# Quartering the token tiles' first products, with a new table of places for every operation

## The chip, the cores and the metric

The kernel runs on one core of one Trainium2 chip. The metric is the device time of one execution in microseconds. Engines are named as in the profile: PE is TensorE (PEld its weight loads), DVE is VectorE, ACT is ScalarE, POOL is GpSimd and SP is SyncE, which issues the DMAs.

## The reference

Attention that keeps the 32 largest scores of each query, and behind it a block that every token passes: two products with a softmax-weighted activation and a layer norm between them.

```python
# q, k, v: (8, 8, 576, 64)
scores = scale * np.matmul(q, k.transpose(0, 1, 3, 2))
kth = np.partition(scores, -32, axis=-1)[..., -32:-31]
scores = np.where(scores >= kth, scores, -1000000000.0)
attn = exp(scores - max); attn /= sum + 1e-09
x = np.matmul(attn, v)                      # -> (4608 tokens, 512)
h = x @ w_in                                # (4608, 1024)
sm = exp(h - max) / (sum + 1e-9)
solu = h * sm
ln = (solu - mean) / sqrt(var + 1e-06) * g_ln
out = ln @ w_out                            # (4608, 512)
```

The weights come as float64 and everything is computed in float32.

## The kernel before

**Attention.** Heads are taken in pairs, four pairs to each of the 8 batches. Of the 576 queries of a batch, 512 form four tiles of 128, and the remaining 64 of two heads fill one more. A step (32 in all, four to a batch) takes two pairs and two query tiles: steps 0 and 1 of a batch do tiles 0 and 1 with pairs 0, 1 and then 2, 3; steps 2 and 3 do tiles 2 and 3. In a step, `scores` (L2216) multiplies queries with keys on PE into PSUM, 64 contraction rows at a time, two matmuls side by side on the upper and lower half of the array; `evac` (L2227) copies the result with ACT. `count0` and `count1` (ACT Sign, DVE compare) count how many scores lie above a moving threshold; `nearest` and `best` (L2312, L2323) find the 16 values nearest to it, from which `kth` picks the 32nd largest. `exps` (L2348) takes exponentials on ACT, `keep` (L2393) zeroes what is below the 32nd on DVE. `transpose_p` (L2470) turns the result on PE, `copy_p` (L2483) copies it, `attn_v` (L2526) multiplies with the values on half the array's columns, two matmuls side by side, and `attn_t` (L2535) adds the last 64 keys. `copy_v` (L2549, L2556) scales the outcome on DVE into `xTm` or `xTt`, which hold x transposed, one slice to each head pair.

**Tokens.** 36 token tiles of 128 (four to a batch, one more for the left-over queries of every second batch) go through `mm1` (L2567, h = x @ w_in, two halves of 512 columns, each a sum over the four head pairs), `hexp` (L2578, ACT), `solu` (L2586, DVE), `square` (L2596, ACT), `spread` and `ln` (POOL), `transpose_ln` (L2617), `copy_ln` (L2623), `mm2` (L2628, two halves of the 1024 rows), `store` (ACT) and `send` (SP). A float32 matmul is two instructions in the trace. The PSUM tile `h` is one of two buffers named "big", and the scores use the same two. While a token's sum is open, until `solu` has read it, the scores have the other one.

**Weights.** 16 chunks are loaded as float64 words; DVE (`w_bits`, `w_corr`) and PE (`w_sum`, L1981) make float32 of them, and `w_copy` puts them into `w_in` (chunks 0 to 7: chunk 2 * pair + half) and `w_out`. At the end they are loaded again and checked.

**What sets the order.** The program of every engine is written out by a planner at build time and is then fixed. `work_of` lists all operations, each with an engine, a duration in ns, an extra time until its result lands (`late`), the operations it comes after and the buffers that it uses. `arranged` goes through them like a simulation: on each engine it looks at the operations whose inputs and buffers can be had, keeps those that could start within `PATIENCE` ns of the earliest of them, and issues the one with the smallest place. Places are the numbers of the table `PLACES` (L778), one for every operation. `TURN` adds ns where PE changes between the whole array ("f"), half the rows ("r", the scores) and half the columns ("c", attn_v). So the table decides between operations, and data decide what it can choose from. Only the order comes out of the planner; on the chip an engine takes its instructions in that order and waits at each for its semaphores.

A second program for inputs that the first cannot treat stands behind a check (`general_path`), and is not executed here.

Of the kernel before, what the change touches and what calls it, by code (L numbers as in the profile page):

```python
# [442 lines left out]
class Work:  # L443
# [6 lines left out]
    def add(self, key, engine, ns, after=(), uses=(), late=0, mode=None):  # L450
# [7 lines left out]
TURN = {("r", "f"): 150, ("f", "r"): 180, ("c", "f"): 205, ("f", "c"): 145,  # L458
        ("r", "c"): 180, ("c", "r"): 180}
# [34 lines left out]
def work_of(B, NP, steps, NF, w_wide):  # L494
# [7 lines left out]
    add = w.add  # L502
# [7 lines left out]
    for b in range(B):  # L510
        for hp in range(NP):
            n = pair(b, hp)
            add(("load_k", n), "SP", 950, behind("load_k", n), [("km", n)], late=2300)
# [11 lines left out]
    for i, (b, chunks) in enumerate(steps):  # L525
# [3 lines left out]
        add(("load_q", i), "SP", 1150, behind("load_q", i), [("q", i)], late=2300)  # L529
# [108 lines left out]
    for m, (b, t, x, made) in enumerate(tokens):  # L638
        for half in range(2):
            ready = made + ([("mm1", m - 1, u) for u in range(2)] if m else []) + [ready_of(c) for c in range(half, 8, 2)]  # L640
            add(("mm1", m, half), "PE", 3480, ready, [x, ("big", ("h", m))], mode="f")
        free = [("w_sum", 15)] if m == 1 and w_wide else []
        add(("hexp", m), "ACT", 1007, free + [("mm1", m, 0), ("mm1", m, 1)], [("big", ("h", m)), ("e", m), ("solu", m)], 115)
# [56 lines left out]
def arranged(work, rank):  # L700
# [23 lines left out]
    while len(start) < len(ops):  # L724
# [56 lines left out]
        -339758, -12781, -25208, -27877, 37731, 233358, 296, 105051, 96218, 90025, 178978, 252902,  # L781
        244000, 268551, 386938, 415275, 391135, 450403, 490825, 467595, 536751, 620389, 565976,
        679127, 740719, 661851, 783898, 770731, 790228, 893927, 893785, 963266,
    ],
    "load_t": [
        -80025, -31145, 36300, 49546, 49494, 80911, 88940, 148972, 157187, 191399, 204618, 265303,
        242814, 379090, 332469, 458214, 479052, 406643, 515896, 540675, 515666, 668938, 671843,
        720581, 717982, 793192, 742027, 827758, 819520, 890032, 913039, 961682,
    ],
    "load_v": [  # L790
        5319, 1480, 51022, 45481, 188816, 144910, 179523, 153830, 308475, 246135, 333153, 327154,
        412030, 463265, 437640, 432012, 583103, 575722, 599884, 559552, 638124, 712663, 704767,
        749478, 828294, 823974, 856710, 843393, 969577, 973661, 982483, 1008016,
    ],
    "prep_t": [
        -61945, -87345, 26278, 19638, -8730, 123415, 112043, 64876, 197393, 203082, 209099,
        243285, 345702, 316325, 405050, 432741, 494037, 489994, 501941, 520044, 617082, 642835,
        681846, 688123, 761106, 717329, 792500, 787155, 909850, 920002, 957331, 948603,
    ],
    "prep_tc": [  # L800
        4338, 31729, 74439, 103211, 71892, 81529, 72919, 101742, 164515, 194340, 295053, 275591,
        364723, 341559, 415389, 407627, 461137, 438553, 503629, 486164, 631436, 665358, 673210,
        709654, 759555, 758129, 786441, 814781, 916829, 948853, 939851, 972581,
    ],
    "prep_k": [
        -60943, -63278, -70349, -26069, -42273, -8750, 127523, 59000, 243742, 222705, 246805,
        237589, 361575, 400598, 401099, 421797, 472374, 488858, 508262, 574786, 637110, 675577,
        651769, 709906, 752064, 690701, 778193, 843688, 919829, 948201, 942202, 976495,
    ],
    "prep_kc": [  # L810
        4386, 1259, 123243, 137096, 118230, 85986, 126740, 91080, 220993, 187701, 233433, 204820,
        376470, 380016, 398731, 436516, 487070, 463318, 479133, 561124, 640742, 660501, 650085,
        710914, 775148, 783534, 778524, 835240, 922803, 1013798, 954303, 988974,
    ],
    "key_square": [
        -4807, -10479, 66029, 137082, 107576, 118285, 100863, 99055, 254747, 223927, 219983,
        241887, 382074, 399900, 389837, 454608, 479887, 488157, 529275, 515189, 644860, 690979,
        690863, 719751, 737841, 761871, 779678, 864903, 916172, 907344, 975895, 1000571,
    ],
    "tail_square": [  # L820
        26929, 14605, 100013, 137131, 136063, 58308, 80392, 79370, 239575, 272229, 246883, 251581,
        308867, 311986, 422199, 446864, 515800, 468069, 496456, 535239, 638456, 682141, 683618,
        672660, 775588, 750923, 772211, 791047, 855138, 930345, 971291, 966358,
    ],
    "key_stats": [
        92348, -19748, 26035, 15202, 122190, 113992, 181544, 108957, 246207, 243025, 253021,
        288772, 408504, 419434, 373738, 411187, 494000, 466874, 543467, 571921, 654056, 667583,
        687366, 699046, 765262, 778703, 806677, 825191, 868806, 1026195, 947557, 979604,
    ],
    "load_q": [  # L830
        -59271, -10584, 162877, 208999, 217746, -8934, 78975, 113377, 212835, 187676, 290008,
        301140, 284434, 326724, 436860, 497003, 414204, 458642, 518992, 564916, 579785, 620846,
        720192, 679914, 758251, 783803, 740037, 850815, 909964, 906235, 929596, 981195,
    ],
    "prep_q": [
        -52938, -38118, 56938, 77044, -59554, 85219, 162709, 142989, 215771, 247729, 278667,
        316160, 380350, 357086, 442926, 462694, 491000, 518228, 547128, 562615, 640425, 655851,
        698990, 730851, 735544, 760091, 823699, 888865, 908286, 923741, 969433, 1014055,
    ],
    "prep_qc": [  # L840
        5438, 63366, 52446, 134767, 64136, 75161, 195035, 183808, 242849, 287460, 293191, 371510,
        425968, 364349, 488763, 476329, 465356, 525184, 499437, 614146, 626301, 699742, 698545,
        745735, 768636, 779604, 840926, 877014, 945804, 930997, 952200, 1033695,
    ],
    "query_square": [
        63169, 84418, 69142, 92064, 62677, 75066, 191341, 120686, 227118, 285294, 276140, 342226,
        401444, 383473, 418081, 451775, 479613, 516395, 563335, 580962, 631937, 667102, 657175,
        748447, 762133, 776709, 773949, 878639, 892717, 939130, 971775, 1057944,
    ],
    "estimate": [  # L850
        -83506, 127952, 79019, 27039, 105930, 180710, 89736, 42838, 243394, 306540, 313101,
        342801, 413707, 436191, 458562, 488897, 502885, 576495, 566964, 582618, 653574, 699822,
        722473, 753711, 782087, 850158, 856146, 880647, 959006, 991084, 1003644, 1011006,
    ],
    "length": [
        55390, 64287, 21492, 142925, 91820, 89828, 187422, 189102, 225343, 302444, 316321, 331213,
        430746, 450075, 467065, 483618, 443843, 521081, 600380, 589002, 638944, 706432, 747530,
        730429, 775752, 832366, 866032, 877201, 961113, 983506, 1018506, 1066670,
    ],
    "root": [  # L860
        99246, 101551, 133489, 76502, 153437, 159993, 328449, 258282, 273277, 322044, 312402,
        345682, 435376, 421796, 426558, 489636, 494032, 574332, 622205, 621698, 663835, 788227,
        724548, 699723, 787574, 869704, 806750, 895189, 992785, 957593, 981899, 1024982,
    ],
    "begin": [
        11137, 56722, 26318, 141798, 82875, 187369, 201720, 176412, 273406, 321410, 278640,
        361581, 425447, 451800, 489085, 488954, 519027, 611009, 600940, 647109, 684366, 701264,
        752228, 758419, 793179, 851495, 882821, 921112, 988338, 1009069, 981779, 1020470,
    ],
    "scores": [  # L870
        [-59418, -45149, -46228, -36187, -85715, -39882, -83465, -59766, -61961],
        [82657, 60941, 68216, 26269, 63090, 61996, 26242, 61177, 58723],
        [87860, 87901, 87890, 62437, 67835, 57982, 159959, 48482, 69765],
        [84367, 83743, 155862, 144031, 34877, 75359, 128841, 135567, 145817],
        [71537, 53849, 68902, 132976, 59114, 118037, 68873, 110264, 107915],
        [141646, 97925, 94716, 134455, 142943, 99507, 191485, 186882, 96824],
        [152938, 191224, 59110, 197551, 203891, 215510, 127964, 202152, 197201],
        [226026, 229460, 237313, 237035, 187502, 187736, 192780, 199624, 198798],
        [269141, 275943, 254553, 254580, 277300, 269126, 277259, 275937, 249924],
        [281479, 298728, 285432, 289527, 294726, 285129, 283716, 304085, 288903],  # L880
        [308491, 308764, 338739, 339201, 342891, 346940, 344779, 346918, 317824],
        [378407, 372124, 377700, 364058, 378360, 351114, 351045, 365023, 349059],
        [417154, 412522, 383108, 385009, 415137, 411709, 389678, 392676, 380697],
        [419351, 419391, 429554, 429553, 450301, 450306, 439041, 439011, 405453],
        [466428, 468152, 464816, 466680, 475154, 473635, 454060, 453530, 452872],
# [353 lines left out]
    ],  # L1239
    "spread_r": [  # L1240
        [61416, 70137],
        [85209, 91923],
        [131370, 129488],
    ],
    "copy_s": [
# [1498 lines left out]
```

## Time and profile before

| | us |
|---|---|
| median of 3 runs | 1195.1 (1193.06 to 1195.21) |
| the profiled execution | 1193.35, span 1191.5 |
| PE busy | 1143.5 (96%) |
| DVE busy | 1054.0 (88%) |
| ACT busy | 1014.4 (85%) |
| POOL busy | 154.4 (13%) |
| mm2 (L2628), 576 matmul instructions, busy | 258.2 |
| mm1 (L2567), 512 and 64 instructions, busy | 229.2 and 28.8 |
| scores (L2216), half rows, 1024 instructions, busy | 169.1 |
| transposes of P (L2470), 1024 instructions, busy | 153.1 |
| attn_v (L2526), half columns, 1024 instructions, busy | 136.1 |

Busy times of an engine are the time in which at least one of its instructions runs. Matmuls overlap (one starts before the one before has left the array), so what a group costs PE is read from the start of it to the start of the next group, not from its durations. The granted clock is the share of TensorE's full clock that the chip's throttle allows.

### The profile page before, as it was taken

How to read it: one execution, taken by the hardware profiler on the slowest of the kernel's cores; microseconds unless marked ns; L12 is line 12 of the kernel's file. 1: busy time of each engine (PE TensorE's matmuls, PEld its weight loads, DVE VectorE, ACT ScalarE, POOL GpSimd, SP SyncE). 2: the span in 40 equal slices, each digit the busy share in tenths (PEclk: the TensorE clock that was granted, in tenths of full speed). 3: DMA queues.
4: the chain of work that ended last, by engine and by line, in shares of the span. 5: the costliest groups of instructions: out<-in, count | busy, mean ns of one | idle time of the engine just before them, and what ended most of it. 6: DMA issues, size and time to landing. Idle time of an engine off the chain costs nothing.

```text
span 1191.5 us, 18863 instructions
## 1 busy us (share of the span) xinstructions
PE 1143.5 (96%) x5868; PEld 648.2 (54%) x5868; DVE 1054.0 (88%) x3113; ACT 1014.4 (85%) x2180; POOL 154.4 (13%) x169
## 2 busy tenths in 40 slices
PE   6689999999999999999999999999999999999997
PEld 3345455555555555555555655555555555555553
DVE  4999999999899999899979998899989888999821
ACT  7899798999988898999896998999877989988642
POOL 1101101102021020202031010211013001120110
PEclk9799999999999999999999999999999999999999
DMA  7323111012110122111120112111020101102521
GB/s 202 97 75 92 43 34 48 13 49 54 59 26 28 33 63 65 37 45 40 51 54 12 40 49 68 31 41 52 30 76 18 42 21 40 59 11 91 173 76 30
DMA packets 110408, 64.55 MB, mean 54 GB/s; under 512 B 89421, under 2 KB 97882, under 8 KB 110298
## 3 DMA queue, kind: packets, MB, share of 16 engines
q1 hardware_dynamic: 110298, 63.25, 18.8%
q8 instruction: 49, 0.80, 0.3%
q14 instruction: 61, 0.50, 0.1%
HBM read 53.65 MB, written 9.57 MB: 53 GB/s over the span
## 4 chain that ended last, share of the span: by engine, by line
PE 50%; DVE 27%; ACT 17%; issue 3%; POOL 2%; DMA 0%; DVEq 0%; ACTq 0%; POOLq 0%
PE o_ps L2628 14%; PE h_ps L2567 9%; PE s_ps L2216 9%; ACT sg L2291 7%; PE tp_p L2470 6%; PE om L2526 6%; DVE junkv L2234 6%; DVE w L2323 5%; DVE w L2312 5%; DVE E L2393 3%; ACT PT L2483 2%; DVE solu L2586 2%; ACT X L2227 2%; PE tp_ln L2617 2%; PE om L2535 2%
## 5 line engine op out<-in xcount | busy, mean ns | idle before, releaser
L2628 PE MATMUL o_ps<-w_out,lnT 128*128 128x512 f32 x576 | 258.2, 594 | 0.2
L2567 PE MATMUL h_ps<-w_in,xTm 128*128 128x512 f32 x512 | 229.2, 593 | 0.0
L2323 DVE MAX8 w<-w 128x8 f32<-128x288 f32 x576 | 223.3, 445 | 0.2
L2291 ACT ACTIVATE sg<-X,t 128x576 bf16<-128x576 f32 x256 | 196.4, 774 | 12.0 <-DVE t L2276 10.8
L2312 DVE SCALAR_TENSOR_TENSOR w<-X,al,sg 128x576 f32<-128x576 f32 x256 | 200.7, 813 | 0.8
L2393 DVE SCALAR_TENSOR_TENSOR E<-X,kth,E 128x576 f32<-128x576 f32 x256 | 199.1, 815 | 1.6
L2227 ACT ACTIVATE X<-s_ps 128x576 f32<-128x576 f32 x256 | 160.2, 661 | 25.0 <-PE s_ps L2216 22.5
L2234 DVE TENSOR_SCALAR_CACHE_REDUCE junkv<-X,t 128x576 bf16<-128x576 f32 x216 | 174.6, 808 | 7.6 <-ACT X L2227 1.5
L2216 PE MATMUL s_ps<-kT,qT 64*128 64x288 f32 x1024 | 169.1, 438 | 9.8 <-ACT X L2227 4.4
L2628 PEld LDWEIGHTS o_ps<-w_out,lnT 128*128 128x128 f32 x576 | 105.1, 190 | 112.4 <-issue 110.1
L2470 PE MATMUL tp_p<-ident,E 128*128 128x128 f32 x1024 | 153.1, 278 | 7.9 <-DVE E L2393 2.9
L2483 ACT COPY PT<-tp_p 128x512 f32<-128x512 f32 x256 | 147.0, 591 | 12.4 <-PE tp_p L2470 11.9
L2470 PEld LDWEIGHTS tp_p<-ident,E 128*128 128x128 f32 x1024 | 116.3, 141 | 65.4 <-issue 31.8
L2348 ACT ACTIVATE E<-X 128x1152 f32<-128x1152 f32 x128 | 149.1, 1183 | 1.4 <-PE tp_p L2470 1.2
L2567 PEld LDWEIGHTS h_ps<-w_in,xTm 128*128 128x128 f32 x512 | 93.3, 190 | 98.1 <-issue 95.7
L2526 PE MATMUL om<-PT,vm 128*64 128x320 f32 (+1 forms) x1024 | 136.1, 411 | 1.0 <-ACT osb L2635 0.9
L2186 POOL TENSOR_TENSOR zs<-zs,phalf 128x9 f32<-128x9 f32 x32 | 63.6, 1989 | 520.2 <-DVE zs L2180 520.2
L2216 PEld LDWEIGHTS s_ps<-kT,qT 64*128 64x128 f32 x1024 | 85.7, 186 | 68.3 <-issue 22.2
L2526 PEld LDWEIGHTS om<-PT,vm 128*64 128x64 f32 x1024 | 69.9, 136 | 54.6 <-issue 10.6
L2602 POOL TENSOR_SCALAR var<-var 128x1 f32<-128x1 f32 x36 | 13.0, 361 | 490.3 <-ACT e_sb L2596 490.1
L2596 ACT ACTIVATE e_sb<-solu,nmu 128x1024 f32<-128x1024 f32 x36 | 41.5, 1153 | 23.1 <-DVE nmu L2590 21.8
L2578 ACT ACTIVATE e_sb<-h_ps 128x1024 f32<-128x1024 f32 x36 | 36.7, 1020 | 20.0 <-PE h_ps L2567 19.7
(146 smaller groups left out, 1503.9 us busy)
## 6 DMA issues: line engine op xcount, KB each, us to landing
km<-in_k_dram SPq DMA_DIRECT2D x32, 256.0 KB
q_sb<-in_q_dram SPq DMA_DIRECT2D x64, 128.0 KB
vm<-in_v_dram SPq DMA_DIRECT2D x32, 256.0 KB
out_dram<-osb SPq DMA_DIRECT2D x32, 256.0 KB
scales<-rows SPq DMA_DIRECT2D x58, 128.0 KB
w_raw<-in_moe_w_in_dram SPq DMA_DIRECT2D x8, 512.0 KB
w_raw<-in_moe_w_out_dram SPq DMA_DIRECT2D x8, 512.0 KB
w_again<-in_moe_w_in_dram SPq DMA_DIRECT2D x8, 512.0 KB
```

The lines of the kernel that those rows point to most:

```text
L2216: nc.tensor.matmul(out=s[:, n, 0:SH], lhsT=queries_of(i, t)[hd, :], rhs=kT[hd, k0 : k0 + SH], start=True, stop=True,)
L2227: nc.scalar.activation(out=x, in_=st[i].pop(("s", j))[:, :, 0:SH], func=AF.Copy, scale=scale,)
L2234: nc.vector.tensor_scalar(out=junk, in0=x_of(i, j), scalar1=st[i][t][:, j : j + 1], scalar2=None, op0=ALU.is_ge, op1=ALU.add, accum_out=co ...
L2291: nc.scalar.activation(out=d["sg", j], in_=x_of(i, j), func=AF.Sign, scale=-(1.0 + 2.0**-23), bias=d["t1"][:, j : j + 1], accum_out=column ...
L2312: nc.vector.scalar_tensor_tensor(out=w, in0=x_of(i, j), scalar=d["al"][:, j : j + 1], in1=d.pop(("sg", j)), op0=ALU.subtract, op1=ALU.mult,)
L2323: nc.vector.max(w8[:, j, 8 * half : 8 * half + 8], w[:, half * SH : (half + 1) * SH])
L2393: nc.vector.scalar_tensor_tensor(out=e, in0=x_of(i, j), scalar=d["kth"][:, j : j + 1], in1=e, op0=ALU.is_ge, op1=ALU.mult, accum_out=den_a ...
L2470: nc.tensor.transpose(tp[:, c, :], e[:, c * P : (c + 1) * P], ident)
L2483: nc.scalar.copy(out=dst, in_=st[i].pop(("tp", j)))
L2526: nc.tensor.matmul(out=o[h * D : (h + 1) * D, cols], lhsT=vm[:, h, c, :], rhs=pt[:, h * NM + c, :], start=(c == 0), stop=False,)
L2567: nc.tensor.matmul(out=h[:, half, :], lhsT=x[:, c, :], rhs=w_in[:, c, half * 512 : (half + 1) * 512], start=(c == 0), stop=(c == NP - 1),)
L2628: nc.tensor.matmul(out=o, lhsT=d["lnT"][:, c, :], rhs=w_out[:, c, :], start=(c == 0), stop=(c == NF - 1),)
```

## The change

It has four parts.

1. `mm1` comes in four operations to a token instead of two. Operation `quarter` adds two head pairs' rows (`two` = 0 or 1: pairs 0, 1 or pairs 2, 3) into one half of the columns (`half`). It is listed as waiting for the `copy_v` of those pairs alone, and for the two weight chunks that it reads. Whichever part of a half comes first opens the sum, and the last closes it. All four parts of a token still come after all parts of the token before. `hexp` waits for the four.
2. Every number in `PLACES` is another one (about 1,000 lines). Shown here are the first of `mm1`, whose rows now have four places.
3. `PATIENCE` goes from 300 (PE), 100 (ACT, DVE, POOL) and 2000 (SP) to 3000 and 10000 ns.
4. The planner's numbers: leaving half rows costs 240 or 270 in place of 150 or 180, going to them 165 or 170 in place of 180, and the loads of K and Q are taken to land 0.6 and 0.3 us later.

No instruction is added to or taken from the work of any engine; only order, and what the waits are for, can differ.

```diff
--- before.py
+++ after.py
@@ -455,8 +455,8 @@
 
 
 HOP = {"PE": 90, "ACT": 40, "DVE": 35, "POOL": 90, "SP": 100}
-TURN = {("r", "f"): 150, ("f", "r"): 180, ("c", "f"): 205, ("f", "c"): 145,
-        ("r", "c"): 180, ("c", "r"): 180}
+TURN = {("r", "f"): 240, ("f", "r"): 165, ("c", "f"): 205, ("f", "c"): 145,
+        ("r", "c"): 270, ("c", "r"): 170}
 PORT = {
     "second", "moved", "side", "nearest", "merged", "which", "chosen", "kth", "kth_size",
     "ends", "keep", "begin", "ln", "key_stats", "w_bits", "w_corr", "w_gain",
@@ -510,7 +510,7 @@
     for b in range(B):
         for hp in range(NP):
             n = pair(b, hp)
-            add(("load_k", n), "SP", 950, behind("load_k", n), [("km", n)], late=2300)
+            add(("load_k", n), "SP", 950, behind("load_k", n), [("km", n)], late=2900)
             add(("load_t", n), "SP", 1800, behind("load_t", n), [("qkt", n)], late=2100)
             add(("load_v", n), "SP", 1750, behind("load_v", n), [("vm", n), (f"vd{n % 4}", n)], late=3000)
             made = [("prep_t", n - 1), ("prep_k", n - 1)] if n else []
@@ -526,7 +526,7 @@
         def p_of(c):
             return pair(b, chunks[1 if c == NM else c][0])
 
-        add(("load_q", i), "SP", 1150, behind("load_q", i), [("q", i)], late=2300)
+        add(("load_q", i), "SP", 1150, behind("load_q", i), [("q", i)], late=2600)
         add(("prep_q", i), "PE", 436, [("load_q", i)], [("q", i), ("tp", ("q", i)), ("qT", i)], mode="f")
         add(("prep_qc", i), "ACT", 465, [("prep_q", i)], [("tp", ("q", i)), ("qT", i)], 135)
         add(("query_square", i), "ACT", 465, [("prep_q", i)], [("tp", ("q", i)), ("q", i)], 135)
@@ -636,11 +636,15 @@
             made = [i for i, (bb, ch) in enumerate(steps) if bb in (b - 1, b)]
             tokens.append((b, NM, ("xTt", b // 2), [("copy_v", i, 0) for i in made]))
     for m, (b, t, x, made) in enumerate(tokens):
-        for half in range(2):
-            ready = made + ([("mm1", m - 1, u) for u in range(2)] if m else []) + [ready_of(c) for c in range(half, 8, 2)]
-            add(("mm1", m, half), "PE", 3480, ready, [x, ("big", ("h", m))], mode="f")
+        for quarter in range(4):
+            two, half = divmod(quarter, 2)
+            ready = [
+                ("copy_v", i, p) for _, i, p in made if steps[i][1][2 * p][0] // 2 == two
+            ] + ([("mm1", m - 1, u) for u in range(4)] if m else [])
+            ready += [ready_of(2 * hp + half) for hp in (2 * two, 2 * two + 1)]
+            add(("mm1", m, quarter), "PE", 1740, ready, [x, ("big", ("h", m))], mode="f")
         free = [("w_sum", 15)] if m == 1 and w_wide else []
-        add(("hexp", m), "ACT", 1007, free + [("mm1", m, 0), ("mm1", m, 1)], [("big", ("h", m)), ("e", m), ("solu", m)], 115)
+        add(("hexp", m), "ACT", 1007, free + [("mm1", m, u) for u in range(4)], [("big", ("h", m)), ("e", m), ("solu", m)], 115)
         add(("solu", m), "DVE", 1480, [("hexp", m)], [("big", ("h", m)), ("e", m), ("solu", m)], 90)
         add(("square", m), "ACT", 1133, [("solu", m)], [("e", m), ("solu", m)], 110)
         add(("spread", m), "POOL", 860, [("square", m)], [("solu", m)])
@@ -778,1005 +782,1005 @@
 
 PLACES = {
     "load_k": [
...
     "mm1": [
-        [153478, 67240],
-        [155877, 40111],
-        [130905, 89746],
-        [62467, 155907],
...
+        [113944, 154004, 119681, 148561],
+        [91178, 137105, 98219, 111195],
+        [195281, 198187, 182937, 195299],
+        [195529, 194521, 196791, 198342],
+        [253632, 259078, 250152, 248412],
+        [265085, 262902, 256986, 261162],
+        [320711, 328332, 327569, 322451],
+        [330809, 329224, 353128, 332549],
...
     ],
 }
-PATIENCE = {"PE": 300, "ACT": 100, "DVE": 100, "POOL": 100, "SP": 2000}
+PATIENCE = {"PE": 3000, "ACT": 3000, "DVE": 3000, "POOL": 3000, "SP": 10000}
 TURNING = 0
 
 
@@ -2560,15 +2564,18 @@
 
 
 
-    def mm1(d, half):
+    def mm1(d, quarter):
+        two, half = divmod(quarter, 2)
         x = d["x"]()
         h = once(d, "h", lambda: ps_big.tile([P, 2, 512], F32, tag="big", name="h_ps"))
-        for c in range(NP):
+        done = once(d, ("summed", half), lambda: [])
+        for c in (2 * two, 2 * two + 1):
             nc.tensor.matmul(
                 out=h[:, half, :], lhsT=x[:, c, :],
                 rhs=w_in[:, c, half * 512 : (half + 1) * 512],
-                start=(c == 0), stop=(c == NP - 1),
+                start=not done, stop=len(done) == NP - 1,
             )
+            done.append(c)
 
     def h_of(d):
         return d["h"].rearrange("p a f -> p (a f)")
```

## The prediction

> **What bounds the kernel now.** I read the page's first two parts first, for the engine that is nearest to full and for when it is not.
>
> ```profile
> PE 1143.5 (96%) x5868; PEld 648.2 (54%) x5868; DVE 1054.0 (88%) x3113; ACT 1014.4 (85%) x2180; POOL 154.4 (13%) x169
> PEclk9799999999999999999999999999999999999999
> ```
>
> TensorE (PE) is busy in 1143.5 of 1191.5 us, so 48 us is all that a better filled order could win. VectorE (DVE) has 137 us to spare, ScalarE (ACT) 177. The granted clock is below nine tenths in one slice, near the start. Then I cut the span into stretches, to see where the 48 us lie.
>
> ```profile
> 0.00:60.00 60.00, 38.27 (x181) 21.39 (x182) 42.86 (x128) 47.89 (x112) 7.06 (x32) 0.86 0.57 148
> 60.00:150.00 90.00, 80.82 (x431) 43.31 (x432) 87.03 (x242) 79.23 (x179) 7.86 (x8) 1.00 0.24 71
> 150.00:1140.00 990.00, 980.18 (x5139) 562.81 (x5137) 914.95 (x2715) 869.47 (x1854) 133.68 (x120) 1.00 0.17 49
> ...
> 1170.00:1191.50 21.50, 14.27 (x41) 6.42 (x39) 0.47 (x4) 4.61 (x10) 1.94 (x3) 0.89 0.14 42
> ```
>
> The columns are the stretch, its length, and busy time of PE, weight loads, DVE, ACT and POOL. PE idles 21.7 us in the first 60, 9.2 in the next 90, 9.8 in the 990 of the middle, and 7.2 in the last row, which is the last store and the verdict. From 1140 to 1170 it doesn't idle. The middle is 99% full: what it loses, it loses while busy. The timeline of PE shows how.
>
> ```profile
> 408.62 3.60 PE L2567 MATMUL h_ps<-w_in,xTm 128*128 128x512 f32 x8
> 412.18 0.66 PE L2470 MATMUL tp_p<-ident,E 128*128 128x128 f32 x4
> 412.68 3.60 PE L2567 MATMUL h_ps<-w_in,xTm 128*128 128x512 f32 x8
> 416.11 1.29 PE L2470 MATMUL tp_p<-ident,E 128*128 128x128 f32 x8
> ...
> 428.49 1.24 PE L2216 MATMUL s_ps<-kT,qT 64*128 64x288 f32 x8
> 429.66 0.66 PE L2617 MATMUL tp_ln<-ident,solu 128*128 128x128 f32 x4
> 430.16 0.60 PE L2092 MATMUL tp_qk<-ident,km 128*128 128x128 f32 x4
> 430.59 0.38 PE L2076 MATMUL pre<-ident,qk_tails 128*128 128x128 f32 x2
> ...
> 431.49 0.66 PE L2617 MATMUL tp_ln<-ident,solu 128*128 128x128 f32 x4
> 432.08 1.30 PE L2216 MATMUL s_ps<-kT,qT 64*128 64x288 f32 x8
> ...
> 436.77 1.14 PE L2216 MATMUL s_ps<-kT,qTt 128*128 128x288 f32 x4
> 437.74 0.60 PE L2470 MATMUL tp_p<-ident,E 128*128 128x128 f32 x4
> ```
>
> The time from one start to the next is what a group costs. Four 288-column matmuls on the whole array cost 437.74 - 436.77 = 0.97 us. Eight on half the rows, two at a time, should cost the same, but between full-array groups they cost 429.66 - 428.49 = 1.17: 0.20 more. Four transposes cost 0.43 (430.16 to 430.59), but between two half-row groups 0.59 (431.49 to 432.08): 0.16 more. So leaving the full array and coming back costs 0.36 us, 0.18 each way. Along PE's matmuls in order of time I count 347 such changes (126 from half rows to full, 111 back, 110 to or from half columns): 62 us that the profile calls busy. That is more than all the idle time.
>
> **The change part by part.**
>
> **The same products in four parts.** A half is 3.43 us (412.68 to 416.11), a quarter 1.72; 36 tokens have the same 576 matmul instructions and weight loads as before. New are 72 places where other work can come in between. Transposes behind a product cost 0.50 (412.18 to 412.68), 0.07 over the 0.43; the product of 408.62, behind a shorter group, took 3.56, 0.13 over. If half of the 72 are used: 36 x 0.07 = 2.5. Ends 0 and 72 x 0.07 = 5; I take **+2**, as neighbours that are moved away save some.
>
> **Parts that can start a step earlier.** A quarter with the first two head pairs' rows waits for one attention step, not two. The timeline of DVE and PE around the first token:
>
> ```profile
> 82.71 0.42 DVE L2549 TENSOR_TENSOR xTm<-om,scales 128x256 f32<-128x256 f32 x1
> ...
> 112.76 0.42 DVE L2549 TENSOR_TENSOR xTm<-om,scales 128x256 f32<-128x256 f32 x1
> 114.63 3.60 PE L2567 MATMUL h_ps<-w_in,xTm 128*128 128x512 f32 x8
> ```
>
> The first product starts 1.5 us after the second step's last copy ends at 113.2. Its first two quarters could start at about 83, and the weights' last copy for w_in starts at 86.8. Between 83.2 and 114.63 PE's gaps add up to 4.1 us, and only token 0 can use them (token 1 waits for all of token 0): at most 2 x 1.72 = 3.4. But the new places of token 0's quarters are 113.9, 154.0, 119.7 and 148.6 (in us), nothing near 83. I take **-1**, ends 0 and -3.4. In the middle the same freedom can fill part of 9.8 us. Pieces half as long fit more gaps, but none of its waits is over 1.3 us, shorter than a quarter. I take **-2**, ends 0 and -5.
>
> **The places and PE's changes of mode.** The new table replaces every place. As a check of what it describes: the old places of the second products lie a median 25 us ahead of their real starts, the new ones 10 us ahead of the same old starts, with quartiles 5 and 15. So the tokens' order is much the old one. Sorting all PE operations by place alone gives 437 changes of mode in the old table (the real order has 347) and 395 in the new. Scaled, 347 x 395 / 437 = 314, 33 fewer: -5.9 us. Against it: with a patience of 3 us in place of 0.3 the planner follows the places more literally, and 395 themselves would be +8.6. The higher TURN prices (240 for half rows to full, where the trace shows about 0.15 to 0.2 us) push the plan to fewer changes. I take **-3**, ends -10 and +9. The Trainium skill (TensorEngine Tiling (Array Packing), Key Properties) says that a change of tiling mode drains the TensorE. Priced by the drain of TensorE: Matmul & The Clock Gate (Step-by-step: about 128 cycles at 2.4 GHz, an estimate of 0.053 us), 33 changes would be worth 1.8 us, my half of it -1, and the whole sum -2 in place of -4; the measured 0.18 decides.
>
> **Patience.** A longer patience lets the plan leave PE idle up to 3 us for an operation of a better place. The rule that speaks against it is that same page's clock gate: idle gaps of more than about 3 us bring the clock back to half. The trace agrees: the stretch of 22.5 to 27.6, with 0.06 us of PE work, was followed by 5.6 us at a clock of 0.50, and the 3.2 us up to 36.4 by 3.6 us at 0.54. So one such wait in the middle costs 3 us and about 2 to 3 more. The middle has none now, and I take none; each one would be +5 to +6.
>
> **SyncE's loads.** The assumed landings of K and Q are 0.6 and 0.3 us later, so the plan issues them earlier. Behind K's first load, which nothing hides, PE waited 1.3 us for Q and 0.7 for the tails: **-1**, ends -2 and 0. The loads' places move too, but SyncE's queue waits several hundred us in sum for free buffers without holding PE.
>
> **PSUM.** A sum that is open over a step holds one of the two "big" buffers, which scores need too. Now PE waits little for that:
>
> ```profile
> PE s_ps L2216 <- ACT X L2227: 4.7, 11, 1.0
> ```
>
> With one buffer, every scores operation must wait for the copy of the one before (0.66 us). I take **+1**, for the few sums that stay open longer; ends 0 and +15.
>
> **Sum:** +2 - 1 - 2 - 3 - 1 + 1 = **-4 us**. The profiled execution took 1193.35 us (span 1191.5 and 1.85 around it), so 1189.4 for its like. It lies 1.75 below the median of the runs shown, 1195.1; against that the same sum is 1191.1. I predict **1190.5**.
>
> **The rivals.**
>
> *Slower, by held PSUM.* For 16 pairs of query tiles (8 batches, two each) a token's sum may open after one step and close after the next, 30 us later as 83 to 113 shows. Nine scores then run on one buffer. If 0.3 us of each 0.66 us copy is not covered, one such stretch costs 2.7 us. Two of the 16 cancel the gain, six give -4 + 16 = 1203. For it: the old plan holds the buffer only some 10 us (two halves, exp and solu). Against: the quarters' places lie close together for most tokens (token 7's are 331, 329, 353 and 333).
>
> *Slower, by more changes of mode.* If the order comes near the 395 that the places give when sorted, +8.6 in place of -3: 1202. It decides from 347 + 5 changes on, where its loss meets the other terms' -1. For it: patience. Against: the dearer TURN.
>
> *No change.* PE is 99% full for 990 us; the order of the tokens stays; all terms are small and may cancel: 1193 to 1197.
>
> *More gain.* A fifth fewer changes of mode, 69 x 0.18 = 12.4, with the other terms at -1: 1182.
>
> **How the numbers follow.** A run of this kernel can be told from another at about 0.2%, 2.4 us: below 1192.7 is faster, over 1197.5 slower. The forecast has 0.36, more gain 0.10, no change 0.13, held PSUM 0.20, more changes of mode 0.21. So faster 0.46, same 0.13, slower 0.41. One in ten is left out on each side: 1182 to 1204. The likeliest case alone, with the changes of mode at -6 or 0 and the filling at its ends, has 1185 to 1192.5.
>
> **What would show it.** Right: changes of mode down to some 310 to 335, PE's idle time in the middle at 7 to 9 us, its clock at 1.00 from 61 us on, waits of scores for ACT's copies at most 6 us, busy PE near 1141. Wrong: more than 352 changes, a stretch in the middle with a clock below 1, idle PE in the middle over 13 us, or scores that wait 10 us and more for ACT. If the first h_ps starts near 85 us, not 115, the early start was worth more than I took.

## The result

The changed kernel takes 1200.01 us (median of 6 runs, 1198.74 to 1200.48) where the kernel before took 1194.11 (6 runs) beside it: a ratio of 1.0043, 95% interval 1.0033 to 1.0053. It is slower by 5.9 us between the medians, or by 5.1 us if the ratio is used, which is not the quotient of the medians. The forecast was 1190.5, faster than before; the time lies inside the range of 1182 to 1204, but on the other side of before. The profiled execution took 1199.99 us, span 1198.2; before it was 1193.35 and 1191.5.

### The profile page after: what moved, and what is told of

The parts are those of the page before. It is cut to its first block, busy times and chain, and to the rows that moved or that the text cites. A ratio compares the mean times of both kernels' runs of the same rounds, so it can differ in the third digit from the quotient of the medians.

```text
span 1198.2 us, 18838 instructions
## 1 busy us (share of the span) xinstructions
PE 1146.3 (96%) x5866; PEld 648.9 (54%) x5868; DVE 1071.0 (89%) x3113; ACT 1024.0 (85%) x2180; POOL 153.1 (13%) x169
## 4 chain that ended last, share of the span: by engine, by line
PE 55%; DVE 25%; ACT 14%; issue 2%; POOL 1%; DMA 1%; SPq 1%; DVEq 0%; ACTq 0%; POOLq 0%
PE o_ps L2635 17%; PE s_ps L2220 9%; PE tp_p L2474 7%; PE om L2530 7%; PE h_ps L2573 7%; DVE junkv L2238 6%; DVE E L2397 5%; ACT sg L2295 4%; DVE w L2316 4%; DVE w L2327 4%; ACT X L2231 3%; PE om L2539 2%; PE tp_ln L2624 2%; PE tp_qk L2096 2%; DVE solu L2593 2%
## 5 line engine op out<-in xcount | busy, mean ns | idle before, releaser
L2573 PE MATMUL h_ps<-w_in,xTm 128*128 128x512 f32 x512 | 232.8, 593 | 0.0
L2327 DVE MAX8 w<-w 128x8 f32<-128x288 f32 x576 | 227.9, 448 | 3.0
L2316 DVE SCALAR_TENSOR_TENSOR w<-X,al,sg 128x576 f32<-128x576 f32 x256 | 205.7, 823 | 2.2
L2530 PE MATMUL om<-PT,vm 128*64 128x256 f32 (+1 forms) x1024 | 136.7, 411 | 0.2
L2630 ACT COPY lnT<-tp_ln 128x512 f32<-128x512 f32 x72 | 41.4, 592 | 17.2 <-PE tp_ln L2624 17.1
L2616 POOL TENSOR_SCALAR solu<-solu,nmu,rstd 128x1024 f32<-128x1024 f32 x36 | 51.9, 1440 | 3.8
```

What stands on the lines that cost most here:

```text
L2316: nc.vector.scalar_tensor_tensor(out=w, in0=x_of(i, j), scalar=d["al"][:, j : j + 1], in1=d.pop(("sg", j)), op0=ALU.subtract, op1=ALU.mult,)
L2327: nc.vector.max(w8[:, j, 8 * half : 8 * half + 8], w[:, half * SH : (half + 1) * SH])
L2530: nc.tensor.matmul(out=o[h * D : (h + 1) * D, cols], lhsT=vm[:, h, c, :], rhs=pt[:, h * NM + c, :], start=(c == 0), stop=False,)
L2573: nc.tensor.matmul(out=h[:, half, :], lhsT=x[:, c, :], rhs=w_in[:, c, half * 512 : (half + 1) * 512], start=not done, stop=len(done) == NP ...
```

## The profile after

The first part of the page and the row of the granted clock:

```profile
PE 1146.3 (96%) x5866; PEld 648.9 (54%) x5868; DVE 1071.0 (89%) x3113; ACT 1024.0 (85%) x2180; POOL 153.1 (13%) x169
PEclk9699999999999999999999999999999999999999
```

PE is busy 2.8 us longer with the same instructions, and the second slice, 30 to 60 us, has a clock of 0.6 where it was 0.7. The same stretches as before (length, then busy time of PE, weight loads, DVE, ACT, POOL, then clock and DMA):

```profile
0.00:60.00 60.00, 38.37 (x170) 20.25 (x171) 40.45 (x121) 45.90 (x105) 7.03 (x32) 0.76 0.53 144
60.00:150.00 90.00, 82.88 (x429) 44.91 (x430) 87.40 (x244) 79.79 (x181) 7.54 (x7) 0.97 0.25 71
150.00:1140.00 990.00, 974.36 (x5099) 559.23 (x5099) 932.50 (x2716) 875.37 (x1848) 132.69 (x121) 1.00 0.17 46
```

PE's idle time is 21.6, 7.1 and 15.6 us, where it was 21.7, 9.2 and 9.8: the middle was to have less and has 5.8 more. The clock of the first two stretches fell from 0.86 and 1.00 to 0.76 and 0.97. Changes of mode, counted as in the prediction, went from 347 to 309, below the 314 that I had scaled from the places. So the count came out and the gain did not.

**Where the middle lost.** The waits of PE in the middle (150 to 1140 us), first before, then after (us in total, times, longest):

```profile
PE tp_ln L2617 <- POOL solu L2609: 2.2, 4, 1.3
PE tp_p L2470 <- ACT PT L2483: 0.8, 4, 0.2
PE s_ps L2216 <- ACT X L2227: 0.8, 3, 0.3
```

```profile
PE s_ps L2220 <- ACT X L2231: 4.6, 18, 0.3
PE tp_ln L2624 <- POOL solu L2616: 2.8, 4, 1.3
PE tp_p L2474 <- ACT PT L2487: 1.7, 3, 1.2
```

3.8 of the 5.8 us are scores (`s_ps`) that wait for ACT's copy; transposes of P and of `ln` wait 0.9 and 0.6 us more. The timeline shows where (start, duration, group, idle time before it):

```profile
502.99 1.24 PE L2220 MATMUL s_ps<-kT,qT 64*128 64x288 f32 x8
504.49 1.30 PE L2220 MATMUL s_ps<-kT,qT 64*128 64x288 f32 x8 [0.26 <-ACT X L2231]
505.72 0.70 PE L2539 MATMUL om<-PT,v_diag 128*128 128x256 f32 x2
```

Four half-row scores operations (x4 each) follow one another without full-array work between them. There are two buffers, and the third operation starts 0.26 us late, when ACT has copied the first: 505.72 - 502.99 = 2.73 us for four. Two runs of two, as in the prediction's timeline of before, cost 2 x 1.17 and once more the 0.16 of coming back, 2.50. Merging two runs of two removes two changes of mode and costs 0.2 us; by the price of the prediction it was to save 0.36. Beyond 4 x 0.485 = 1.94 us (0.485 is half of the 0.97 us of the prediction's full-array scores), the four take 0.79 us. Of these, 0.26 show as idle time; what makes the rest, the trace does not say.

The whole middle, read from start to start along PE's matmuls; "beyond nominal" is what a run takes above 0.485 us for each operation until the next full-array group starts:

| half-row operations in one run | runs before | runs after | mean beyond nominal, before, us | after, us |
|---|---|---|---|---|
| 1 | 26 | 12 | 0.24 | 0.27 |
| 2 | 91 | 71 | 0.25 | 0.23 |
| 3 | 1 | 3 | 0.81 | 0.75 |
| 4 | 2 | 11 | 0.81 | 0.84 |
| 6 and 8 | 0 | 2 | | 1.35, 1.89 |
| all | 120 | 99 | sum 31.0 | sum 34.2 |

With 21 fewer runs the sum rose by 3.2 us. A single operation joined to another single saves; a pair joined to a pair does not. The table leaves out the 0.16 us of coming back behind each run, 21 x 0.16 = 3.4 us less by estimate. So the runs as a whole came out even, where 38 fewer changes at 0.18 us were to save 6.8.

**Where the start lost.** The timeline of after's start:

```profile
23.08 0.39 PE L1986 MATMUL w_tp<-w_tmp,ident 128*128 128x512 bf16 x1
25.83 2.04 PE L1985 MATMUL w_tp<-w_tmp,ident 128*128 128x512 f32 x2 [2.37 <-DVE step L2264]
...
30.81 0.63 PE L1986 MATMUL w_tp<-w_tmp,ident 128*128 128x512 bf16 x1
36.46 1.12 PE L2096 MATMUL tp_qk<-ident,q_sb 128*128 128x128 f32 x4 [5.02 <-ACT w_in L1992]
...
46.74 6.01 PE L2220 MATMUL s_ps<-kT,qT 64*128 64x288 f32 x24
...
60.71 1.97 PE L2474 MATMUL tp_p<-ident,E 128*128 128x128 f32 x8 [1.53 <-DVE E L2397]
```

From 24.9 to 52.2 us PE has half the clock: four transposes take 1.12 us, where at full clock they take 0.60 to 0.66. The first transposes of P start at 60.71; before they started at 57.52, and half clock lay in 26.4 to 33.3, 36.7 to 40.1 and 53.7 to 60.6. In sum, by the trace's records of the granted clock and without the end of the span, half clock went from 17 to 37.5 us; the changed kernel has further pieces of it at 59.0 to 65.8 and 151.2 to 154.6.

## The experiments

Each kernel's ratio is to the kernel before, run on the same chip beside it (1194.0 to 1194.8 us in the five groups). An interval reaches about 0.1%, some 1.2 us, to each side, so smaller differences between two kernels are not told apart.

| run | what it is | median, us | ratio, 95% interval |
|---|---|---|---|
| e1 | changed, with before's first 70 us | 1197.03 | 1.0020 (1.0013 to 1.0027) |
| e2 | before, with the changed first 70 us | 1195.74 | 1.0006 (0.9997 to 1.0014) |
| e3 | before's order, quarters | 1194.43 | 1.0003 (0.9995 to 1.0011) |
| e4 | changed, token 0 waits for both steps | 1199.99 | 1.0052 (1.0038 to 1.0066) |
| e5 | before, runs of scores merged | 1198.98 | 1.0037 (1.0024 to 1.0051) |
| e6 | changed, long runs cut | 1198.61 | 1.0034 (1.0023 to 1.0046) |
| e7 | e1, long runs cut | 1195.53 | 1.0008 (0.9999 to 1.0016) |
| e8 | changed, start kept busy | 1196.66 | 1.0018 (1.0010 to 1.0025) |
| e9 | before, start kept busy, too long | 1197.67 | 1.0035 (1.0023 to 1.0047) |
| e10 | e6 with e8's products | 1194.49 | 1.0005 (0.9996 to 1.0014) |
| e11 | e1, order searched anew | 1195.13 | 1.0014 (1.0005 to 1.0023) |
| e12 | changed, order searched anew, kept busy | 1195.87 | 1.0019 (1.0010 to 1.0028) |
| e13 | before, products fitted | 1191.31 | 0.9980 (0.9971 to 0.9989) |
| e14 | changed, products fitted | 1193.96 | 1.0003 (0.9994 to 1.0012) |
| e15 | e6, products fitted | 1194.31 | 1.0003 (0.9994 to 1.0012) |
| e16 | e11, products fitted | 1195.18 | 1.0007 (0.9998 to 1.0016) |
| e17 | e5, products fitted | 1199.30 | 1.0040 (1.0026 to 1.0054) |
| e18 | e1, products fitted | 1195.70 | 1.0012 (1.0003 to 1.0021) |

### Start, rest and quarters apart

In e1, e2 and e3 the places are the start times (in ns) of an order put together from the two plans, which a patience of 3000 makes the planner keep. The places of `mm1` for token 0, first in e1 against the changed kernel, then in e3 against before:

```diff
 PLACES = {
...
-        [113944, 154004, 119681, 148561],
+        [77787, 118333, 110643, 115939],
...
-        [153478, 67240],
+        [114062, 109022, 115802, 110762],
```

**e1** has before's operations up to 70 us and the changed order behind.

> The changed kernel, with the order of the kernel before for everything that its plan starts in the first 70 us, and the changed order behind it. Theory START (most of the 5.9 us goes in the first 76 us, where PE ran 27 us at half clock and the first step's attn_v came 6 us later): 1194 to 1196.5 us, and the trace has the first attn_v near 70 us, as before. Theory MIDDLE (the waits of PE between 150 and 1140 us, 15.6 against 9.8, cost it): 1199 to 1201. Theory QUARTERS (token 0's sum, open for 41 us, keeps a PSUM buffer from the scores): 1199 to 1201.

**e2** is its counterpart in before, still with halves.

> The mirror of it: the kernel before, with the changed order for what that plan starts in the first 70 us, and its own order behind it; first products in halves. START: 1198 to 1200 us. MIDDLE and QUARTERS: 1193 to 1195.5.

**e3** has before's order on every engine and the changed `mm1`.

> The order of the kernel before on every engine, with the first products in quarters that may start a step earlier where PE has room (token 0's first two do). QUARTERS: 1197 to 1201 us. START and MIDDLE: 1193 to 1195.5, within 0.15% of the kernel before.

**e4** is the changed kernel without the early start of token 0.

```diff
-                ("copy_v", i, p) for _, i, p in made if steps[i][1][2 * p][0] // 2 == two
+                ("copy_v", i, p) for _, i, p in made if m == 0 or steps[i][1][2 * p][0] // 2 == two
```

> The changed kernel, where token 0's four quarters wait for both steps, so that its sum is open for 12 us instead of 41; the order of everything else is kept. QUARTERS: 1195 to 1197.5 us. START and MIDDLE: 1199 to 1202 (the early quarter had filled at most 1.7 us).

The quarters by themselves are not the cause (e3), nor is the sum of token 0 that stays open (e4: no gain or loss that shows, though its five runs spread from 1197.7 to 1202.2). e1 lies between the ranges of START and MIDDLE: the order behind 70 us costs about 2.2 us over before. The new start costs 3.0 us in front of the changed rest (1200.0 against e1) but only 0.9 in front of the old rest (e2), so the parts do not simply add.

### Long runs of scores

Here the order is written out, and the places are ranks in it.

```diff
 def arranged(work, rank):
+    return sorted(work.ops, key=rank)
```

**e5** merges ten pairs of runs in before. PE's order at one of them:

```diff
 ('scores', 16, 0)
 ('scores', 16, 1)
+('scores', 16, 3)
+('scores', 16, 2)
 ('transpose_ln', 13, 1)
 ('transpose_ln', 13, 0)
 ('attn_t', 14, 0)
-('scores', 16, 3)
-('scores', 16, 2)
 ('attn_v', 14, 1)
```

> Before's order, with pairs of neighbouring runs of two half-row scores made into one run of four at ten more places of the middle (the full-array work between them moved behind or ahead). Runs of four go from 2 to 12, changes of PE's mode from 347 to 332. Theory CHANGES (what my prediction used: each change of mode removed is worth 0.18 us): 15 x 0.18 = 2.7 us less, 1191.5 to 1192. Theory RUNS (a run of four takes 2.68 us from its start to the next full-array group, two runs of two take 2 x 1.17 and about 0.15 for the second way in, because the third operation waits until ScalarE has copied the first out of one of the two buffers): each place costs 0.2 to 0.33 us, 2 to 3.3 us more, and up to 1 us for the work that was moved: 1196 to 1198.5.

**e6** does the reverse in the changed kernel.

```diff
-('transpose_p', 9, 7)
 ('scores', 10, 2)
 ('scores', 10, 4)
+('transpose_p', 9, 7)
 ('scores', 10, 6)
 ('scores', 10, 7)
```

> After's order, with its runs of three or more half-row scores in the middle cut into runs of two at sixteen places, by one or two full-array operations moved in between. Runs of four and more go from 13 to 2, changes of mode from 309 to 341. CHANGES: 32 x 0.18 = 5.8 us more, about 1205.5. RUNS: 16 x 0.2 to 0.33 = 3.2 to 5.3 us less, of which I leave 1 us to the moved work: 1195.5 to 1198, and the waits for ScalarE ahead of scores in the middle fall from 4.6 us towards 1.

**e7** makes the same cuts in e1.

> The same sixteen cuts in the kernel of the earlier run that had before's order for the first 70 us and the changed order behind (1197.0). CHANGES: 1202.5. RUNS: 1193.5 to 1195.5, the time of before, since then neither the start nor the long runs are left of the change.

Fewer changes made before slower by 4.7 us (e5), well clear of noise. More changes made the changed order 1.4 us faster in e6, where the intervals overlap, and 1.5 us faster in e7 than in e1, where they just do. All three exclude CHANGES, which forecast 1191.5 to 1192, 1205.5 and 1202.5. RUNS had the direction right, but was 0.5 us too low in e5, 0.6 in e6, and e7 ended at the upper edge of its range. The waits of PE in the middle, in e5 and then in e6 (L1300 and L1304 are the scores there, L1311 and L1315 ACT's copies):

```profile
PE s_ps L1300 <- ACT X L1311: 4.3, 14, 0.6
```

```profile
PE s_ps L1304 <- ACT X L1315: 2.3, 6, 0.9
```

Merging takes them from 0.8 to 4.3 us, cutting from 4.6 to 2.3.

### The clock of the start

```diff
+    def warm(times):
+        t = ps_o.tile([P, 512], F32, tag="o", name="warm")
+        for _ in range(times):
+            nc.tensor.matmul(out=t[:, 0:P], lhsT=ident, rhs=ident, start=True, stop=True)
+
...
+    WARM = {('w_sum', 2): 16, ('w_sum', 4): 30, ('prep_t', 3): 14}
...
+            if key in WARM:
+                warm(WARM[key])
```

**e8** adds them to the changed kernel.

> The changed kernel with 70 products of the identity with itself that nobody reads, put on TensorE into the waits of its start: 16, 30 and 14 behind the third and fifth converted weight chunks and the fourth pair's tails, 10 behind the fourth step's estimate (about 0.11 us each at full clock). The order of all other work is unchanged. Theory CLOCK (the new start is slower because TensorE is given half clock from 24.9 to 52.2 us): the half-clock time falls from about 37 us to 15 or less, and the total by 2 to 4 us, to 1196 to 1198. Theory ORDER (the start is slower because of what its order waits for, and the clock only follows): 1199.5 to 1201, whatever the clock does. If the products only push the work behind them, 1201 to 1203.

The edit has 10 more products behind the fourth step's estimate, in free columns of its own tile. 3.4 us less, as CLOCK said. The clock of the first 60 us is 1.00 in the trace, and the first transposes of P start at 58.13.

**e9** does it in before.

> The kernel before with 88 products of the identity with itself that nobody reads in three waits of its start: 42 behind the scores ahead of the 5 us wait, 24 behind the third pair's tails, 22 behind the fourth step's estimate. Theory CLOCK: in the changed kernel the same means took about 34 us of half clock away and 3.4 us of time, 0.1 us for each; here 17 us of half clock can go, so 1.7 us: 1192 to 1193.5. If the gain there came from something else in the changed start, 1194 to 1195 here. If the products push the work behind them: over 1195.

It became slower. The timeline of e9:

```profile
22.16 9.64 PE L2679 MATMUL warm<-ident 128*128 128x128 f32 x84
...
34.82 5.52 PE L2679 MATMUL warm<-ident 128*128 128x128 f32 x48
...
63.02 0.60 PE L2475 MATMUL tp_p<-ident,E 128*128 128x128 f32 x4
```

42 products are 84 instructions and fill 9.64 us of a wait of 5.1. I had counted one instruction for each. The transposes of P came 5.5 us late, at full clock. So e9 shows what it costs to push the work back, 6.4 us against e13, whose products fit the waits and whose first 60 us have the same clock, 0.97.

**e10** puts the cuts and the products together.

> The changed kernel with both repairs: the sixteen cuts of its long runs of scores and the 70 products in the waits of its start. If the two causes are separate, their gains add: 1200.0 - 1.4 - 3.4 = 1195.2, so 1194.5 to 1196. If the clock's gain was in part the long runs', or the other way round, 1196.5 to 1198.5.

5.5 us less than the changed kernel, a little more than the sum of the two gains, 4.8.

**e11** and **e12** take other prices for the planner and a new order under them.

```diff
-                add(("scores", i, j), "PE", 485 if t < NM else 970,
+                add(("scores", i, j), "PE", 586 if t < NM else 970,
...
-TURN = {("r", "f"): 240, ("f", "r"): 165, ("c", "f"): 205, ("f", "c"): 145,
+TURN = {("r", "f"): 30, ("f", "r"): 110, ("c", "f"): 205, ("f", "c"): 145,
```

> The order of the kernel with before's first 70 us and the changed order behind (1197.0), rearranged by many small moves that were kept when they shortened the planned order under prices read from the traces: 0.586 us in place of 0.485 for a half-row scores operation, 0.03 and 0.11 us for leaving and entering half rows in place of 0.24 and 0.165, and a buffer of the scores that comes free 0.14 us later. The search was not told to avoid long runs; it left none over two, and 355 changes of mode in place of 310. CHANGES: 45 x 0.18 = 8 us more, 1205. RUNS: at least as good as the sixteen cuts by hand, 1194 to 1195.5; if the prices are also right for the rest of the order, below before, 1189 to 1193.

> The changed kernel's own order, rearranged in the same way (349 changes of mode, two runs of four left in the middle), with the 70 products in the waits of its start. CHANGES: 1196.7 + 40 x 0.18 = 1204. RUNS and CLOCK together: 1195.2 or less; if the prices are right for the rest of the order too, 1188 to 1193, below both kernels.

e11 gains 1.9 us over e1, about as much as cutting by hand (1.5). e12 is 1.4 us slower than e10 and above the 1195.2 that both theories together allowed. So the corrected prices avoid long runs, and this search under them found no better order.

**e13** to **e16** have the products fitted to the waits: 20, 11 and 10 for before's start, 8, 20, 6 and 5 for the changed one.

> As the run with products in before's start, but sized to the waits: each product takes 0.23 us (two instructions of 0.114), so 20, 11 and 10 in place of 42, 24 and 22 for waits of 5.1, 3.0 and 2.9 us. Theory CLOCK: before's 17 us of half clock in the start cost it time too; without them the first product with V starts before 70.0 us and the total is 1192 to 1193.3. Theory ORDER: half clock costs before nothing because ScalarE and VectorE set the end of its start; 1193.5 to 1194.5.

> The changed kernel with 8, 20, 6 and 5 products, fitted to its waits of 2.4, 5.0, 1.8 and 1.5 us. CLOCK: at least the gain of the 70 (which ran 1 to 2 us past the waits): 1195.5 to 1197. If the gain there came from anything but the clock, 1198 to 1200.

> The sixteen cuts and the fitted products in the changed kernel. CLOCK and RUNS as separate causes: 1193.5 to 1195, before's time within 0.1%. If the start still costs something of its own: 1195 to 1196.5.

> The order searched under the measured prices behind before's start (1195.1), with the products fitted to before's waits. CLOCK: 1.5 to 2 us less, 1193 to 1193.7, before or a little below it. ORDER: 1194.7 to 1195.5.

e13 is faster than both kernels, by 3.0 us over before. The first 60 us of e13 and of e14 have a clock of 0.97, where before had 0.86 and the changed kernel 0.76:

```profile
0.00:60.00 60.00, 45.30 (x280) 29.42 (x281) 45.21 (x133) 49.49 (x116) 7.05 (x32) 0.97 0.56 149
```

```profile
0.00:60.00 60.00, 43.23 (x261) 28.17 (x263) 44.40 (x132) 49.73 (x116) 7.03 (x32) 0.97 0.55 148
```

The timeline of e13:

```profile
21.58 4.73 PE L2679 MATMUL warm<-ident 128*128 128x128 f32 x40
26.73 0.66 PE L2092 MATMUL tp_qk<-ident,q_sb 128*128 128x128 f32 x4 [0.42 <-ACT kT L2103]
...
55.49 0.60 PE L2475 MATMUL tp_p<-ident,E 128*128 128x128 f32 x4
```

The products end 0.42 us before the data come, and P's transposes start at 55.49 instead of 57.52. In the changed kernel the same means bring 6.05 us (e14). So the half clock of the start costs 3.0 us in before and 6.0 in the changed kernel: about 3 us of the 5.9. CLOCK forecast too small a gain in both. The same program shows the tie too: e3's nine runs at a mean clock of 0.990 took 1193.9 to 1194.7 us, its four at 0.985 or 0.986 took 1197.2 to 1198.3.

The cuts bring nothing on top of the fitted products: e15 has 1194.31 against 1193.96 in e14. It ended in the range for two separate causes only because e14 had gained more than forecast. In e15's trace PE's idle time in the middle is 12.5 us, in e14's 14.7, but there are 34 more changes of mode in it. e16 ends where e11 did, as ORDER said, though its mean clock rose from about 0.989 to 0.994: with the same start and the same products as e13, it gains nothing.

**e17** and **e18** put the long runs alone and the changed order behind 70 us alone on e13's start.

> Before's order with ten more runs of four scores (332 changes of mode in place of 347) and the products fitted to before's waits, so that both this and the kernel that it is compared with (fitted products alone, 1191.3) are at full clock nearly all the time. CHANGES: 15 x 0.18 = 2.7 us less, 1188.6. RUNS: the 4.7 us that the same merging cost at half clock were the runs and the waits that they bring, not the clock: 1195 to 1196.5. If a part of them was the clock: 1192.5 to 1194.5.

> Before's order for the first 70 us, the changed order behind it, and the products fitted to before's waits. Against the fitted before (1191.3) it differs only in the order behind 70 us. If the changed order of the middle costs what the two traces at full clock show (5.2 us more idle, 2.0 us less lost at changes), 3.2 us: 1193.5 to 1195. If the middle's loss was the clock too, 1191 to 1192.5.

The middle of e13, e17 and e18 at full clock:

```profile
150.00:1140.00 990.00, 980.66 (x5125) 562.55 (x5125) 912.47 (x2709) 867.19 (x1851) 133.60 (x120) 1.00 0.17 49
```

```profile
150.00:1140.00 990.00, 976.49 (x5113) 559.45 (x5111) 911.08 (x2705) 865.41 (x1848) 133.70 (x120) 1.00 0.17 48
```

```profile
150.00:1140.00 990.00, 974.93 (x5111) 558.96 (x5111) 929.68 (x2709) 877.14 (x1851) 131.54 (x120) 1.00 0.17 47
```

PE's idle time is 9.3, 13.5 and 15.1 us. Up to 150 us e13 and e17 agree within 0.2 us of PE's busy time, so e17's profiled execution (1194.71 against 1189.46) isolates the ten merged places and the work moved for them: 5.2 us more, 0.5 for each place, twice what the run itself costs; the idle time is 4.2 of it. Its five runs spread from 1194.7 to 1200.5 us, the longer ones with a lower granted clock, so its median lies above what RUNS said. At an equal mean clock the difference stays: 1194.7 and 1196.7 at 0.997 or 0.998 against e13's 1189.5 to 1191.3 at 0.997, and 1199.7 and 1200.5 at 0.992 against 1195.1.

e18 is 4.4 us above e13 and 0.7 above its range. Its clock is a little lower; at an equal one it is 3 to 4 us above (1194.3 against 1189.5 to 1191.3 at 0.997, 1196.2 to 1196.8 against 1193.1 at 0.994). So the changed order behind 70 us costs time of its own at full clock. How much of it the long runs cost is not settled: merging ten pairs costs before 5 us, but cutting the long runs gives the changed order at most 2.2 us back.

## Why the prediction was wrong

- **Quarters, +2:** nothing in before's order; e3 has +0.3 us, interval -0.6 to +1.3. There the products of all tokens but the first stand together as before's do, in 71 pieces with other work of PE between them where before had 69. In the changed kernel's trace they stand in 100; what the 31 more cost was not tried alone.
- **Early start, -1:** the first quarter started at 86.8, near the earliest that I had named, but it fills waits that nothing then needed: e4 takes it away at no cost that shows.
- **Filling of the middle, -2:** wrong sign. The idle time went from 9.8 to 15.6 us, above the 13 that I had named as a sign of error. A second such sign came too, a stretch below full clock in the middle (151.2 to 154.6 us).
- **Changes of mode, -3: the step that failed.** 309 is even fewer than the forecast's 314, and 0.18 us for each change was measured where a run of two scores stands between full-array groups. I carried that price to changes that go away when two runs become one. For singles it holds; for pairs the third operation waits for one of two buffers and the price turns round, to +0.2 us for the run alone (the timeline) and about +0.5 with what moves (e17). From e13 to e18 in the middle, 41 fewer changes were to save 7.4 us by that price. They brought about 2 us less lost in busy time, and 5.7 us more idle time, of which the scores' waits for ACT are 3.8 (0.8 to 4.6).
- **Patience and the clock: the missing term.** I priced waits of 3 us in the middle and took none, and left the half clock of the start as it stood, at nothing and without a reason. In the changed order it doubled, from 17 to 37.5 us, for about 3 us of time.
- **Landings, -1:** not tried alone. Of the waits that it was to remove, the 1.3 us for Q are gone from the changed kernel's trace, the 0.7 for the tails are not.
- **PSUM, +1:** the resource was right, the holder wrong. Not an open token sum (e4; in the trace only token 0's products spread over 41 us, those of every other token over 7 to 14) but the scores themselves hold both buffers. The rival "held PSUM" came near in its time, 1203, by luck: its mechanism did not occur, and -4 + 16 counted from 1194.5, the forecast without its -4, makes 1206.5. The rival "more changes of mode" is excluded by the count.

The terms, from the runs near full clock: the order behind 70 us +4.4 (e18 - e13), the new start -1.7 (e14 - e18), and the clock of the start +3.1 (6.05 - 2.97), 5.8 in sum. The sum is no check, since it follows from how the terms are taken. Each is known to 1 or 2 us only, since the gains of the same edit differ with what is around it: the products bring 6.0 us in the changed kernel, 3.0 in before, 1.3 in e1 and nothing in e11, the last three with the same start; the cuts bring 1.4, 1.5, 2.2 and nothing. So the price of half clock is not one number, and what else in the changed order costs PE the remaining idle time stays open.

DVE is busy 17 us longer in every kernel with the changed order behind 70 us (1070 to 1072 us, against 1053 to 1054 in every one with before's), with the same 3113 instructions. Most of it is not slower work. Added up one by one, the durations make 1260.3 us before and 1265.7 after; busy time counts only once where an instruction starts before the last one has ended, and these overlaps are 206.3 and 194.7 us. It was not tried whether PE waits for that.

## What to carry to other kernels

A measured price per event holds for the sequence in which it was measured. Before counting fewer mode changes as gain, ask what a longer run waits for: here runs of two operations, as many as there are PSUM buffers, lost the least for each operation. And look at the clock of the start too: in before, 41 products that nobody reads, fitted to three waits, were worth 3.0 us, and 88 that overran them cost 3.7. With another order behind the same start they were worth 1.3 us or nothing, so this has to be tried in each order.

## What the runs showed of the hardware

The clock falls on less than a long wait. In the changed kernel it fell at 151.2 us after the first of these stretches, and at 24.9 after the last; the second is the one ahead of the first:

```profile
147.80:151.20 3.40, 1.71 (x12) 0.85 (x10) 3.40 (x10) 3.40 (x9) 2.84 (x3) 1.00 0.01 2
144.40:147.80 3.40, 3.40 (x16) 1.55 (x15) 3.37 (x9) 3.40 (x9) 0.00 (x0) 1.00 0.26 57
21.50:24.90 3.40, 1.50 (x4) 0.40 (x3) 3.33 (x9) 3.33 (x9) 0.00 (x0) 1.00 0.85 259
```

PE was busy in 1.71 of 3.40 us ahead of the fall at 151.2, where the longest single wait was 1.3 us, and in 1.50 of 3.40 ahead of the one at 24.9. The other traces agree. Up to 1180 us, the clock records of the 20 traces cut the time at full clock into 6768 stretches of 3.41 us. PE was busy for at most 53% in each of the 47 that the clock fell behind, and for at least 50% in each of the 6721 others. The Trainium skill (TensorE: Matmul & The Clock Gate, HAM oscillation) warns of idle gaps of more than about 3.4 us; here several short waits that add up to half of such a stretch were enough. So in this case the busy share of 3.4 us is the thing to read, and I had looked for single waits only.
